# Sixteen products of zeros ahead of the third unit's scores in a fused linear-attention and gated-MLP kernel

## The chip, the cores and the metric

The program runs on one core of a Trainium2 chip. The metric is the device time of one execution in microseconds; with several runs the median is taken.

## The reference, cut to what matters

The kernel computes a linear attention with a forget gate per key channel, for 4 batches of 8 heads, 768 tokens and 48 channels, and feeds its output (4 x 768 x 384) into a gated MLP whose gate mixes tokens:

```python
f = 1.0 / (1.0 + np.exp(-f_logit))
for t in range(S):
    state = f[:, :, t, :, None] * state + np.einsum('bhd,bhe->bhde', k[:, :, t], v[:, :, t])
    y[:, :, t] = np.einsum('bhd,bhde->bhe', q[:, :, t], state)

h = np.maximum(x @ w_in, 0.0)
u, v = (h[..., :d_ff // 2], h[..., d_ff // 2:])
v_n = (v - mu) / np.sqrt(var + 1e-06)
v_s = np.einsum('ts,bsd->btd', w_spatial, v_n) + b_spatial[None, :, None]
return (u * v_s) @ w_out
```

## The kernel before, in words

The attention is cut into 24 units of 128 tokens (4 batches of 6 units), each in two chunks of 64. The order of all work is written out by hand: PLAN is a list of words such as `X:2`, and each word calls one step function with its numbers. Every engine takes its own instructions in the order in which the words stand, so a word's place sets its place in the queue of each engine that it uses.

One unit n goes through these steps. `LF`, `LK` and `LQ` load its gate logits, keys and queries, and values (lines 325 to 337, on the queue of SP); `c` clamps the logits (line 341), `e` takes exp and log (lines 345 and 346), `z` sums them along the tokens, for the first six units as products with a triangular matrix on TensorE (line 356), later as a scan on VectorE (line 351). `h` and `g` are the exponentials of the sums (lines 362 and 367), `k` and `q` scale keys and queries on VectorE (lines 373 and 377). `X` are the scores, 32 small products (line 401); `m` masks them on VectorE (line 411), `w` copies their other half on ScalarE (line 407). `YS` and `kv` are products with the values (lines 453 and 425), `r0`, `r1` and `r2` update the state (lines 433, 439 and 444), `Yq` adds the state's part of the output (line 465), `ys` copies the output (line 468), `xt` transposes it on TensorE with three products (line 477), and `xh` and `xl` split it into two parts (lines 487 and 492). The buffers of a unit's logits, keys and queries go round in threes, so that unit 6 may be loaded only when unit 3's scores have been read.

Beside the units the plan loads and splits the weights (`LV`, `LU`, `LW`, `ca`, `ct`, `ch`, `cl`, `wh`, `wl`), and from unit 4 on it weaves in the products of the MLP (`V`, `U`, `S`, `P`, `O`; lines 513, 619, 633, 664 and 818).

The word `D:n` issues n products of `junk` with itself on TensorE: `junk` is a tile of bf16 zeros set at the start, each product is 128 by 128 by 256, and its result goes to the bank that `W0` takes and `W1` gives back; nobody reads it. Each product comes with a load of its weights. The plan before has `D:11`, `D:29` and `D:3` (lines 49 to 51), and `W1` stands in line 52, behind the place of the change:

```python
def step_D(count):
    for _ in range(count):
        nc.tensor.matmul(mm.of("warm")[:, 0:2 * P], junk[:, 0:P], junk[:, 0:2 * P], start=True, stop=True)
```

Around the change the words that use TensorE are, in order: `Yq:1 xt:0 X:2 xt:1 z:4 YS:2 kv:2 X:3`. VectorE has `k:2 r2:1 q:2` ahead of the scores and `m:2 wl:1,1 k:3 r0:2` behind them. SP has `LQ:4 LF:6 LK:5 LU:0` behind `X:3`.

Of the kernel before, what the change touches and what calls it, by code (L numbers as in the profile page):

```python
# [10 lines left out]
F32 = mybir.dt.float32  # L11
# [7 lines left out]
B, H, S, D = 4, 8, 768, 48  # L19
# [10 lines left out]
P = 128  # L30
KX = HD // P
KS = S // P
KG = G // P
HK = KS // 2
TH = S // 2
# [7 lines left out]
HELD = FAST[:-1]  # L43
# [5 lines left out]
    constants LF:0 LF:1 units:1 W0 c:1 c:0 e:0 units:0 D:11 LF:2 c:2 e:1 z:0 LQ:1 LV:0 g:0 z:1 LK:0 h:0 k:0 q:0 LK:1 g:1  # L49
    h:1 k:1 fm:1 D:29 q:1 LQ:0 X:0 m:0 e:2 ca:V,0 LV:1 ct:V,0 LF:3 X:1 LF:4 w:0 c:3 YS:0 LK:3 kv:0 c:4 r0:0 ca:V,1 z:2  # L50
    r1:0 w:1 LK:4 Yq:0 r2:0 m:1 YS:1 e:4 e:3 LQ:2 LK:2 ys:0 ct:V,1 ch:V,0 D:3 kv:1 LQ:3 r0:1 r1:1 z:3 g:2 fm:0 h:2 k:2
    r2:1 q:2 fm:2 h:3 g:3 cl:V,0 Yq:1 LW:1,1 xt:0 LW:2,0 X:2 LF:5 c:5 ys:1 xt:1 fm:3 W1 z:4 q:3 m:2 wh:1,1 wl:1,1 LW:1,0
    YS:2 k:3 ch:V,1 w:2 kv:2 xh:0 e:5 wh:2,0 r0:2 X:3 g:4 LU:1 LW:0,1 cl:V,1 xl:0 runs m:3 LQ:4 Yq:2 r1:2 r2:2 z:5 w:3
    LF:6 c:6 wl:2,0 LK:5 h:4 LU:0 YS:3 ys:2 kv:3 k:4 fm:4 xh:1 wh:0,1 r0:3 q:4 V:0,0 r1:3 X:4 LF:7 ca:U,1 xl:1 xt:2 w:4
    ct:U,1 m:4 g:5 Yq:3 r2:3 e:6 k:5 wh:1,0 V:0,1 z:6 h:5 xh:2 LB YS:4 kv:4 ys:3 xt:3 q:5 xl:2 vr:0,1 r0:4 r1:4 ca:U,0
    vr:0,0 X:5 LQ:5 ch:U,1 Yq:4 c:7 fm:5 wl:1,0 wl:0,1 V:0,2 r2:4 w:5 m:5 YS:5 cl:U,1 ys:4 h:6 g:6 q:6 LW:2,1 LQ:6 xh:3
    vr:0,2 xt:4 k:6 xl:3 e:7 kv:5 xh:4 nm:0,0 X:6 r0:5 LF:9 Yq:5 z:7 vc:0,2 vc:0,1 xl:4 LF:8 LQ:7 V:0,3 r1:5 ys:5 xt:5
    m:6 V:0,4 sq:0,2 c:9 ct:U,0 sq:0,1 c:8 vc:0,0 xh:5 xl:5 sq:0,0 LW:0,0 h:7 YS:6 fm:7 na:0,0 nb:0,0 ch:U,0 V:0,5 q:7
    nc:0,0 g:7 w:6 k:7 kv:6 X:7 cl:U,0 vh:0,2 r0:6 Yq:6 vh:0,0 vl:0,0 U:0,0,3 vl:0,2 m:7 e:8 z:8 r1:6 vh:0,1 vl:0,1
    vr:0,4 bs:0,4 vr:0,3 U:0,1,3 w:7 ur:0,1,3 r2:6 YS:7 fm:6 vr:0,5 bs:0,3 bs:0,5 ys:6 na:0,1 h:8 q:8 kv:7 e:9 U:0,0,2  # L60
    r0:7 LF:10 nb:0,1 nc:0,1 ur:0,0,3 vn:0,5 xt:6 g:8 k:8 r1:7 wh:2,1 U:0,0,0 vn:0,3 LQ:8 wh:0,0 U:0,0,1 vn:0,4 c:10 X:8
    fm:8 xh:6 xl:6 vh:0,3 wl:0,0 vl:0,3 vh:0,4 Yq:7 V:1,0 ys:7 w:8 vh:0,5 m:8 vl:0,4 YS:8 vl:0,5 kv:8 ur:0,0,2 vr:1,0
    r2:7 z:9 xt:7 LF:11 LQ:9 xh:7 xl:7 h:9 r0:8 g:9 wl:2,1 e:10 r1:8 S:0,0,2 moe sg:0,0,2 LO:1 r2:8 k:9 q:9 S:0,0,1
    ur:0,0,1 Yq:8 bs:1,0 vs:1,0 ys:8 fm:9 z:10 h:10 sg:0,0,1 X:9 g:10 xt:8 sm:0,0,1 V:1,1 m:9 k:10 YS:9 w:9 q:10
    sh:0,0,1 kv:9 r0:9 X:10 ca:O,1 Yq:9 S:0,0,3 ys:9 LF:13 c:11 e:11 xh:8 r1:9 xl:8 V:1,2 r2:9 vr:1,1 LF:12 S:0,1,3
    ct:O,1 ch:O,1 sl:0,0,1 z:11 sm:0,0,2 ur:0,0,0 sg:0,0,3 m:10 fm:10 sm:0,0,3 LQ:11 xt:9 LQ:10 h:11 g:11 k:11 S:0,0,0
    vr:1,2 sg:0,1,3 q:11 bs:1,2 c:12 w:10 YS:10 kv:10 X:11 r0:10 Yq:10 cl:O,1 LO:0 m:11 sh:0,0,2 e:12 w:11 S:0,1,0 r1:10
# [87 lines left out]
def tile_kernel(ctx, tc, fkq, fn, vv, w_cv, w_spT, b_sp, out):  # L155
    nc = tc.nc
# [6 lines left out]
    pairs = pair_pool.enter_context(tc.tile_pool(name="pairs", bufs=1, space=PSUM, reuse_waits="tile"))  # L163
    dram = ctx.enter_context(tc.tile_pool(name="dram", bufs=1, space=bass.MemoryType.DRAM))
    held_v = {(b, u): dram.tile([P, G], F32, name=f"held_v{b}{u}") for b in HELD for u in range(NU)}
    held_u = {(b, th, c): dram.tile([P, TH], F32, name=f"held_u{b}{th}{c}") for b in HELD for th in range(2) for c in range(KG)}

    def tiles(pool, name, count, shape, dtype=F32):
        return [pool.tile(shape, dtype, name=f"{name}{i}") for i in range(count)]
# [17 lines left out]
    runs = attn.tile([DP, J * T], F32, name="runs")  # L187
# [735 lines left out]
    with tc.If(n_bad > 0, preferred_fallthrough_block=True, label="again"):  # L923
        xd = dram.tile([B, HD, S], F32, name="xd")
        with tc.tile_pool(name="steps", bufs=2) as sp:
# [5 lines left out]
            with tc.For_i(0, B) as b:  # L931
                for j, e in ((j, e) for j in range(J) for e in range(2)):
                    f, k, q = (sp.tile([D, NU, T], F32, tag="in", name="in", bufs=3) for _ in range(3))
# [7 lines left out]
                    f, k, q = (t.rearrange("d u t -> d (u t)") for t in (f, k, q))  # L941
# [10 lines left out]
                    for d in range(D):  # L952
                        kv = sp.tile([D, S], F32, name="kv")
# [96 lines left out]
```

## Time and profile before

| | us |
|---|---|
| median of 3 runs | 345.08 (344.42 to 346.0) |
| profiled execution, its own time | 346.77 |
| its span, first to last instruction | 345.3 |
| TensorE busy with products in the span | 330.2 (96%) |
| VectorE busy | 248.9 (72%) |
| ScalarE busy | 186.5 (54%) |
| GpSimd busy | 130.7 (38%) |

Times in the trace are counted from the first instruction. PE is TensorE, DVE VectorE, ACT ScalarE, POOL GpSimd and SP the queue that issues the transfers. The granted clock of TensorE is given as a share of full speed; it has two levels, 1.2 and 2.4 GHz, so 0.50 is the low one and a value between them is a stretch with both. The record of the clock holds its changes, and shows 1.00 ahead of the first one.

### The profile page before, as it was taken

What the parts mean: (1) busy time and instruction counts of PE and PEld (TensorE: products, weight loads), DVE (VectorE), ACT (ScalarE), POOL (GpSimd) and SP (SyncE); (2) the same over time, 40 slices, a digit from 0 to 9 for tenths busy, and PEclk for the clock granted to TensorE, in tenths of its full rate; (3) what the DMA queues carried; (4) which work ended last, traced back from release to release, by engine and by line L of the source; (5) the groups of instructions that cost most, each with busy time, mean ns of one, the idle gap of its engine ahead of it and who ended that gap; (6) DMA issues with size and microseconds to landing.
All of it is one profiled execution on the core that took longest, in us unless ns stands there. A gap on an engine that the chain in (4) does not pass through costs nothing.

```text
span 345.3 us, 10672 instructions
## 1 busy us (share of the span) xinstructions
PE 330.2 (96%) x4535; PEld 303.5 (88%) x4535; DVE 248.9 (72%) x474; ACT 186.5 (54%) x391; POOL 130.7 (38%) x128
## 2 busy tenths in 40 slices
PE   6859999999999999999999999899999999999995
PEld 5647777988999889899888999799999999999995
DVE  2677999998667876768859798977859595773420
ACT  7566799885455476558678464422344144341242
POOL 3113344313055243824235073148341466930500
PEclk9996999999999999999999999999999999999999
DMA  6978937334621839455674384451111022100022
GB/s 222 311 261 245 344 113 252 116 118 123 235 88 30 285 121 332 168 201 163 248 245 146 119 294 150 138 169 46 48 68 47 25 91 91 48 1 25 23 91 76
DMA packets 23573, 51.07 MB, mean 148 GB/s; under 512 B 2400, under 2 KB 14944, under 8 KB 23520
## 3 DMA queue, kind: packets, MB, share of 16 engines
q1 hardware_dynamic: 23520, 50.34, 43.4%
q8 instruction: 36, 0.59, 0.7%
q14 instruction: 17, 0.14, 0.1%
HBM read 39.32 MB, written 11.01 MB: 146 GB/s over the span
## 4 chain that ended last, share of the span: by engine, by line
PE 81%; DVE 7%; DMA 6%; ACT 2%; issue 1%; SPq 1%; POOL 1%; DVEq 0%; ACTq 0%; POOLq 0%
PE mm L619 11%; PE mm L513 10%; PE bank L818 10%; PE mm L664 8%; PE mm L818 7%; PE mm L633 6%; PE bank L664 6%; PE bp L401 6%; DMA fkq<-fkq 4%; PE bp L453 4%; PE bank L619 3%; PE bp L465 3%; PE mm L477 3%; PE bp L425 2%; PE bank L513 2%; DMA val<-vv 1%
## 5 line engine op out<-in xcount | busy, mean ns | idle before, releaser
L649 POOL TENSOR_TENSOR uT<-gt,uT 128x384 f32<-128x384 f32 x21 | 24.9, 1188 | 42.1 <-DVE gt L830 22.4
L341 POOL TENSOR_SCALAR fkq<-fkq 112x512 f32<-112x512 f32 (+1 forms) x15 | 24.6, 1640 | 42.8 <-DMA fkq<-fkq 24.1
L373 DVE SCALAR_TENSOR_TENSOR fkq<-fkq 112x512 f32<-112x512 f32 x24 | 19.1, 796 | 11.7 <-DMA fkq<-fkq 7.1
L401 PE MATMUL bp<-q,fkq 48*64 48x112 f32 x768 | 24.4, 266 | 2.7 <-DVE q L377 2.3
L657 DVE TENSOR_TENSOR gl<-uT,gh 128x384 fp32r<-128x384 f32 x27 | 15.9, 603 | 12.4 <-ACT gh L653 12.3
L401 PEld LDWEIGHTS bp<-q,fkq 48*64 48x64 f32 x768 | 19.7, 137 | 5.2 <-DVE q L377 3.0
L351 DVE TENSOR_TENSOR_SCAN fkq<-runs,fkq 112x512 f32<-112x512 f32 x18 | 22.1, 1230 | 2.1 <-ACT fkq L346 2.0
L444 POOL TENSOR_TENSOR sA<-sA,F 112x192 f32<-112x192 f32 x11 | 8.8, 804 | 37.9 <-DVE sA L439 25.8
L453 PEld LDWEIGHTS bp<-val,sc 64*64 64x64 f32 x768 | 14.0, 137 | 8.0 <-issue 4.4
L572 POOL TENSOR_SCALAR vr_fast<-vr_fast,mv,rs 128x512 f32<-128x512 f32 x7 | 17.7, 2529 | 8.8 <-DVE rs L567 5.4
L411 DVE TENSOR_TENSOR sc<-bp,mask 128x512 f32<-128x512 f32 x24 | 16.4, 684 | 4.7 <-PE bp L401 2.9
L653 ACT CAST gh<-uT 128x384 fp32r<-128x384 f32 x27 | 13.4, 512 | 11.7 <-POOL uT L649 8.0
L407 ACT COPY W<-bp 128x384 f32<-128x384 f32 x24 | 11.4, 474 | 14.2 <-DVE sc L411 13.3
L619 PE MATMUL mm<-xTh,w_inh 128*128 128x384 f32 x75 | 18.9, 360 | 0.0
L513 PE MATMUL mm<-w_inh,xTh 128*128 128x512 f32 x60 | 18.3, 413 | 0.0
L345 ACT ACTIVATE fkq<-fkq 112x512 f32<-112x512 f32 (+1 forms) x24 | 14.5, 606 | 6.8 <-POOL fkq L341 4.1
L453 PE MATMUL bp<-val,sc 64*64 64x48 f32 x768 | 17.0, 226 | 1.3 <-ACT W L407 0.7
L362 ACT ACTIVATE F<-fkq 112x512 f32<-112x512 f32 x18 | 11.4, 634 | 11.4 <-DVE fkq L351 6.5
L468 ACT COPY ysb<-bp 128x384 f32<-128x384 f32 x24 | 11.5, 477 | 11.0 <-PE bp L465 7.5
L619 PE MATMUL mm<-xTh,w_inl 128*128 128x384 f32 x75 | 17.1, 336 | 0.0
L619 PE MATMUL mm<-xTl,w_inh 128*128 128x384 f32 x75 | 17.1, 336 | 0.0
L513 PE MATMUL mm<-w_inh,xTl 128*128 128x512 f32 x60 | 17.0, 392 | 0.0
(245 smaller groups left out, 985.1 us busy)
## 6 DMA issues: line engine op xcount, KB each, us to landing
fkq<-fkq SPq DMA_DIRECT2D x18, 768.0 KB, 5.1
val<-vv SPq DMA_DIRECT2D x24, 192.0 KB, 5.0
out<-osb SPq DMA_DIRECT2D x24, 192.0 KB, 2.0
words<-w_cv SPq DMA_DIRECT2D x4, 768.0 KB, 8.2
fkq<-fkq SPq DMA_DIRECT2D x6, 512.0 KB, 7.1
held_u<-uT SPq DMA_DIRECT2D x15, 192.0 KB, 4.2
uT<-held_u SPq DMA_DIRECT2D x12, 192.0 KB, 2.5
held_v<-vr SPq DMA_DIRECT2D x7, 256.0 KB, 5.4
```

The lines of the kernel that those rows point to most:

```text
L341: other("c", n, nc.vector).tensor_scalar(f, f, -LOGIT_MOST, None, op0=ALU.max)
L351: return nc.vector.tensor_tensor_scan(f[0:DP], runs, f[0:DP], 0.0, op0=ALU.mult, op1=ALU.add)
L373: other("k", n, nc.vector).scalar_tensor_tensor(k, f, 1.0 / F_LEAST, k, op0=ALU.min, op1=ALU.mult)
L401: nc.tensor.matmul(sc[to, e, cs], k[dr, at:at + C], qs[n % 2][dr, j, chunk], start=True, stop=True)
L453: nc.tensor.matmul(y[to, e, cs], s[rows, keys[e]], v[rows, hd], start=j == 0, stop=False, skip_group_check=True)
L513: nc.tensor.matmul(acc, xs[:, c, ut * P:(ut + 1) * P], ws[:, c, G:FF], start=i == 0, stop=i == 3 * KX - 1)
L572: other("vn", (b, u), nc.vector).tensor_scalar(vr, vr, mean(b, th)[:, ut, 0:1], scale(b, th)[:, ut:ut + 1], op0=ALU.subtract, op1=ALU.mult)
L619: nc.tensor.matmul(acc[:, 0:TH], ws[:, kx, cs], xs[:, kx, :], start=i == 0, stop=i == 3 * KX - 1)
L633: nc.tensor.matmul(acc[:, 0:TH], vns.of((b, ks))[va][:, cs], w_sp_s[wb][:, ks, th * TH:(th + 1) * TH], start=i == 0, stop=i == 3 * KS - 1,)
L649: nc.gpsimd.tensor_tensor(uT, gts.of((b, th, c)), uT, op=ALU.mult)
L664: nc.tensor.matmul(acc[:, 0:DM], gs.of((b, th, c))[ga][:, ts], w_out_s[wb][:, c, :], start=c == cs[0] != LAST_C and ga == wb == 0, stop=c ...
L818: nc.tensor.matmul(acc, vns.of(user(i))[va][:, cs], w(i)[wb], start=n == 0 and k in (1, 2, 7), stop=n == 3 * HK - 1, skip_group_check=True)
```

## The change

`D:16` is put into the plan between `LW:2,0` and `X:2`, so on TensorE behind `xt:0` and ahead of the scores of unit 2, the third unit. The diff also makes the dictionary of DRAM buffers `held_u` for one batch more; those tiles are never written or read. Everything else of the diff is the same words in lines broken anew.

```diff
-    r2:1 q:2 fm:2 h:3 g:3 cl:V,0 Yq:1 LW:1,1 xt:0 LW:2,0 X:2 LF:5 c:5 ys:1 xt:1 fm:3 W1 z:4 q:3 m:2 wh:1,1 wl:1,1 LW:1,0
+    r2:1 q:2 fm:2 h:3 g:3 cl:V,0 Yq:1 LW:1,1 xt:0 LW:2,0 D:16 X:2 LF:5 c:5 ys:1 xt:1 fm:3 W1 z:4 q:3 m:2 wh:1,1 wl:1,1
...
-    held_u = {(b, th, c): dram.tile([P, TH], F32, name=f"held_u{b}{th}{c}") for b in HELD for th in range(2) for c in range(KG)}
+    held_u = {(b, th, c): dram.tile([P, TH], F32, name=f"held_u{b}{th}{c}") for b in range(B - 1) for th in range(2) for c in range(KG)}
```

## Rows read from the trace of the kernel before

**Rows 1.** The page: busy time by engine, and the granted clock in 40 slices.

```profile
PE 330.2 (96%) x4535; PEld 303.5 (88%) x4535; DVE 248.9 (72%) x474; ACT 186.5 (54%) x391; POOL 130.7 (38%) x128
...
PEclk9996999999999999999999999999999999999999
```

**Rows 2.** Waits of PE, whole span: total us, times, longest us.

```profile
PE mm L818 <- DVE t3l L740: 1.1, 1, 1.1
...
PE mm L477 <- ACT ysb L468: 0.5, 1, 0.5
...
PE bp L425 <- issue: 0.3, 1, 0.3
```

**Rows 3.** Chain that ended last: start us, us, what.

```profile
32.33 6.15 DMA fkq<-fkq
...
50.15 1.00 PE bp L401 x32
```

**Rows 4.** Stretches: us, busy PE PEld DVE ACT POOL, PEclk, DMA share, GB/s.

```profile
24.40:24.60 0.20, 0.00 (x0) 0.00 (x0) 0.20 (x2) 0.00 (x0) 0.00 (x0) 0.69 0.52 184
...
25.40:31.20 5.80, 5.80 (x111) 4.86 (x115) 3.81 (x5) 4.53 (x9) 2.44 (x4) 0.50 0.86 256
31.20:31.40 0.20, 0.20 (x20) 0.20 (x16) 0.00 (x0) 0.20 (x1) 0.00 (x0) 0.74 0.97 369
```

**Rows 5.** Timeline of PE, 23 to 32 us: start, us, line, tiles, count [idle before].

```profile
23.91 0.38 PE L477 MATMUL mm<-ident,ysb 128*128 128x128 f32 x2 [1.12 <-issue]
25.34 1.77 PE L401 MATMUL bp<-q,fkq 48*64 48x112 f32 x32 [1.05 <-DVE q L377]
27.04 0.90 PE L477 MATMUL mm<-ident,ysb 128*128 128x128 f32 x3
27.87 1.97 PE L356 MATMUL mm<-tri,fkq 128*64 128x128 f32 x16
29.77 1.11 PE L453 MATMUL bp<-val,sc 64*64 64x48 f32 x32
30.66 0.82 PE L425 MATMUL bp<-val,W 64*48 64x48 f32 x32
31.30 0.96 PE L401 MATMUL bp<-q,fkq 48*64 48x112 f32 x32
```

**Rows 6.** Timeline of PE, the same steps of later units at the full clock.

```profile
32.64 1.09 PE L356 MATMUL mm<-tri,fkq 128*64 128x128 f32 x16
34.40 0.68 PE L453 MATMUL bp<-val,sc 64*64 64x48 f32 x32 [0.68 <-ACT W L407]
34.91 0.54 PE L425 MATMUL bp<-val,W 64*48 64x48 f32 x32
...
37.65 1.00 PE L401 MATMUL bp<-q,fkq 48*64 48x112 f32 x32
38.58 0.55 PE L477 MATMUL mm<-ident,ysb 128*128 128x128 f32 x3
```

**Rows 7.** Timeline of PE, the first 12 us.

```profile
2.34 2.53 PE L892 MATMUL mm<-junk 128*128 128x256 bf16 x11 [2.34 <-DVE rescale L231]
5.13 3.17 PE L356 MATMUL mm<-tri,fkq 128*64 128x128 f32 x32 [0.26 <-ACT fkq L346]
8.23 3.34 PE L892 MATMUL mm<-junk 128*128 128x256 bf16 x29
```

**Rows 8.** Timeline of DVE, 27 to 32 us.

```profile
27.18 0.69 DVE L411 TENSOR_TENSOR sc<-bp,mask 128x512 f32<-128x512 f32 x1 [0.42 <-PE bp L401]
...
28.65 0.99 DVE L373 SCALAR_TENSOR_TENSOR fkq<-fkq 112x512 f32<-112x512 f32 x1
31.55 0.36 DVE L433 TENSOR_TENSOR sB<-bp,sA 112x192 f32<-112x192 f32 x1 [1.91 <-PE bp L425]
```

**Rows 9.** The stretch behind unit 3's scores, columns as in rows 4.

```profile
32.00:32.60 0.60, 0.60 (x44) 0.58 (x36) 0.60 (x1) 0.08 (x1) 0.00 (x0) 1.00 0.40 86
```

**Rows 10.** The page: queues, packets, MB, share of 16 engines.

```profile
q8 instruction: 36, 0.59, 0.7%
```

More of the change, by code (lines that the diff above doesn't have):

```diff
@@ L51 @@
     r1:0 w:1 LK:4 Yq:0 r2:0 m:1 YS:1 e:4 e:3 LQ:2 LK:2 ys:0 ct:V,1 ch:V,0 D:3 kv:1 LQ:3 r0:1 r1:1 z:3 g:2 fm:0 h:2 k:2
-    r2:1 q:2 fm:2 h:3 g:3 cl:V,0 Yq:1 LW:1,1 xt:0 LW:2,0 X:2 LF:5 c:5 ys:1 xt:1 fm:3 W1 z:4 q:3 m:2 wh:1,1 wl:1,1 LW:1,0
-    YS:2 k:3 ch:V,1 w:2 kv:2 xh:0 e:5 wh:2,0 r0:2 X:3 g:4 LU:1 LW:0,1 cl:V,1 xl:0 runs m:3 LQ:4 Yq:2 r1:2 r2:2 z:5 w:3
-    LF:6 c:6 wl:2,0 LK:5 h:4 LU:0 YS:3 ys:2 kv:3 k:4 fm:4 xh:1 wh:0,1 r0:3 q:4 V:0,0 r1:3 X:4 LF:7 ca:U,1 xl:1 xt:2 w:4
-    ct:U,1 m:4 g:5 Yq:3 r2:3 e:6 k:5 wh:1,0 V:0,1 z:6 h:5 xh:2 LB YS:4 kv:4 ys:3 xt:3 q:5 xl:2 vr:0,1 r0:4 r1:4 ca:U,0
@@ L56 @@
[L56 to L64, printed above, removed]
+    r2:1 q:2 fm:2 h:3 g:3 cl:V,0 Yq:1 LW:1,1 xt:0 LW:2,0 D:16 X:2 LF:5 c:5 ys:1 xt:1 fm:3 W1 z:4 q:3 m:2 wh:1,1 wl:1,1
@@ new lines @@
+    LW:1,0 YS:2 k:3 ch:V,1 w:2 kv:2 xh:0 e:5 wh:2,0 r0:2 X:3 g:4 LU:1 LW:0,1 cl:V,1 xl:0 runs m:3 LQ:4 Yq:2 r1:2 r2:2
+    z:5 w:3 LF:6 c:6 wl:2,0 LK:5 h:4 LU:0 YS:3 ys:2 kv:3 k:4 fm:4 xh:1 wh:0,1 r0:3 q:4 V:0,0 r1:3 X:4 LF:7 ca:U,1 xl:1
+    xt:2 w:4 ct:U,1 m:4 g:5 Yq:3 r2:3 e:6 k:5 wh:1,0 V:0,1 z:6 h:5 xh:2 LB YS:4 kv:4 ys:3 xt:3 q:5 xl:2 vr:0,1 r0:4 r1:4
+    ca:U,0 vr:0,0 X:5 LQ:5 ch:U,1 Yq:4 c:7 fm:5 wl:1,0 wl:0,1 V:0,2 r2:4 w:5 m:5 YS:5 cl:U,1 ys:4 h:6 g:6 q:6 LW:2,1
+    LQ:6 xh:3 vr:0,2 xt:4 k:6 xl:3 e:7 kv:5 xh:4 nm:0,0 X:6 r0:5 LF:9 Yq:5 z:7 vc:0,2 vc:0,1 xl:4 LF:8 LQ:7 V:0,3 r1:5
@@ new lines @@
+    ys:5 xt:5 m:6 V:0,4 sq:0,2 c:9 ct:U,0 sq:0,1 c:8 vc:0,0 xh:5 xl:5 sq:0,0 LW:0,0 h:7 YS:6 fm:7 na:0,0 nb:0,0 ch:U,0
+    V:0,5 q:7 nc:0,0 g:7 w:6 k:7 kv:6 X:7 cl:U,0 vh:0,2 r0:6 Yq:6 vh:0,0 vl:0,0 U:0,0,3 vl:0,2 m:7 e:8 z:8 r1:6 vh:0,1
+    vl:0,1 vr:0,4 bs:0,4 vr:0,3 U:0,1,3 w:7 ur:0,1,3 r2:6 YS:7 fm:6 vr:0,5 bs:0,3 bs:0,5 ys:6 na:0,1 h:8 q:8 kv:7 e:9
+    U:0,0,2 r0:7 LF:10 nb:0,1 nc:0,1 ur:0,0,3 vn:0,5 xt:6 g:8 k:8 r1:7 wh:2,1 U:0,0,0 vn:0,3 LQ:8 wh:0,0 U:0,0,1 vn:0,4
+    c:10 X:8 fm:8 xh:6 xl:6 vh:0,3 wl:0,0 vl:0,3 vh:0,4 Yq:7 V:1,0 ys:7 w:8 vh:0,5 m:8 vl:0,4 YS:8 vl:0,5 kv:8 ur:0,0,2
@@ L65 @@
+    vr:1,0 r2:7 z:9 xt:7 LF:11 LQ:9 xh:7 xl:7 h:9 r0:8 g:9 wl:2,1 e:10 r1:8 S:0,0,2 moe sg:0,0,2 LO:1 r2:8 k:9 q:9
+    S:0,0,1 ur:0,0,1 Yq:8 bs:1,0 vs:1,0 ys:8 fm:9 z:10 h:10 sg:0,0,1 X:9 g:10 xt:8 sm:0,0,1 V:1,1 m:9 k:10 YS:9 w:9 q:10
     sh:0,0,1 kv:9 r0:9 X:10 ca:O,1 Yq:9 S:0,0,3 ys:9 LF:13 c:11 e:11 xh:8 r1:9 xl:8 V:1,2 r2:9 vr:1,1 LF:12 S:0,1,3
```

## The prediction, made before the changed kernel was run

> **What bounds the kernel now.** I read the page first. TensorE is busy 330.2 us of the span of 345.3, and the granted clock is full but for one slice of the 40, the fourth [rows 1]. The list of TensorE's waits comes next: it stands still some 10 us in all, nearly all of it ahead of 50 us; behind 50 us the largest wait is 1.1 us at line 818 [rows 2]. So from 50 us on TensorE is the bound, and what an early edit is worth is what it moves of the start of unit 6's scores, at 50.15 us in the chain of waits [rows 3]. Ahead of that the chain goes through a transfer of 6.15 us from 32.33 us on, unit 6's logits, keys and queries, which is issued when unit 3's scores have been read [rows 3]. The change acts in front of that: the point to watch is the start of unit 3's scores, at 31.30 us [rows 5].
>
> The stretch around the change shows two things. TensorE ends the transposes of unit 0 at 23.91 + 0.38 = 24.29 us and waits 1.05 us for the scaled queries, until 25.34 [rows 5]. And the clock falls in this pause: the slice from 24.40 to 24.60 has a mean of 0.69, which of the two levels 1.00 and 0.50 makes a fall at 24.48 us; it is back in the slice that has 0.74, at 31.30 us, after TensorE has worked without a gap since 25.34 [rows 4, 5]. In these 6 us five steps run at the low level: scores of unit 2, transposes, sums, and the two sets of products with the values. They take 1.77 + 0.90 + 1.97 + 1.11 + 0.82 = 6.57 us [rows 5]; the same steps of later units take 1.00 + 0.55 + 1.09 + 0.68 + 0.54 = 3.86 us at the full level [rows 6], a ratio of 1.70. From the first one's start to the start of unit 3's scores they need 31.30 - 25.34 = 5.96 us, since each begins while the one before it drains; at the full level that is 5.96 / 1.70 = 3.5 us. So the low clock costs 2.5 us there, and the change can win no more than a part of it.
>
> **The change part by part.** Nothing is removed and nothing is moved on any queue but TensorE's; the extra DRAM tiles issue nothing. The added products wait for nothing: the zeros were set at the start, the bank is held already, and TensorE itself was its last writer. They do add a delay for what stands behind them on TensorE.
>
> The price of one: 29 took 3.34 us, so 0.115, and 11 at the start took 2.53 us, 0.23 each, which by the factor of two is the low level (the record of the clock shows nothing ahead of its first change) [rows 7]. A row includes the way of its last product through the array, so I take 0.11 and 0.22 us. They can start at 24.29, right behind the transposes. At the full clock sixteen take 16 x 0.11 = 1.76 us and end at 26.05, 0.7 us behind the present start of the scores; at the low one the end is later.
>
> Whether the clock still falls is the first open cost. It falls 0.19 us after the added products would begin, and TensorE had stood still for 1.12 us just ahead of the transposes [rows 4, 5]. I take it that the fall follows from what lies ahead of 24.29 and still comes at 24.48. Then 0.19 us of them run at the full level (1.7 products), and the other 14.3 take 14.3 x 0.22 = 3.15 us, to 27.63 us, if the clock doesn't rise under them. That is 2.3 us later than the scores start now.
>
> When the clock rises is the second open cost. Two rises can be read. In the stretch here it came 5.96 us after the work became gapless. At the start, 32 products of sums took 3.17 us [rows 7]; at the low level 16 of them take 1.97, 0.123 each [rows 5], at the full one 1.09, 0.068 each [rows 6]; (3.17 - 32 x 0.068) / 0.055 = 18 were slow, so the rise came at 5.13 + 18 x 0.123 = 7.35 us: 2.2 us after the pause of 0.26 us, and 5.0 after the first product of zeros [rows 7]. With the added products the gapless work begins at 24.29, so the rise would come between 24.29 + 2.2 = 26.5 and 24.29 + 6.0 = 30.25 us. The start is the nearer row, since there too zeros come first and other work follows; the mean of its two readings, 3.6 us, gives 27.9.
>
> The sum, as the start of unit 3's scores against 31.30 now:
> - rise at 27.9 (taken): the zeros end at 27.63, 0.27 us at the low level do 0.16 of the 3.5 us, and 27.9 + 3.34 = 31.24. That is 0.06 us earlier: the second half of the slow stretch is won back, and the zeros have eaten it.
> - rise at 26.5: 10.8 zeros are done by then, the rest take 0.57 us, to 27.07, and 27.07 + 3.5 = 30.57, 0.73 us earlier.
> - rise at 30.25: 2.62 us at the low level do 1.54, and 30.25 + 1.96 = 32.21, 0.91 us later.
>
> VectorE doesn't undo the taken case: unit 2's mask starts now at 27.18 and unit 3's keys end at 28.65 + 0.99 = 29.64, 2.46 us later [rows 8]. With scores that end near 28.75 the mask starts there and the keys are ready at 31.2, just when TensorE wants them. The cover is VectorE's pause of 1.91 us ahead of the state's update at 31.55 [rows 8]; gone, it would cost its excess one for one. ScalarE's copies behind the mask move by the same 1.5 us, and the products with the values wait for them only from about 30.2 us on, when the sums have ended.
>
> Behind unit 3's scores all goes on as now, so the profiled execution of 346.77 us (1.47 us more than its span) becomes 346.7. The median of the runs, 345.08, is 1.7 us below that execution; I put the difference to the median: 345.08 - 0.06 = 345.0 us.
>
> One cost lies in code. The core fetched instructions 36 times, 0.59 MB [rows 10], 16 KB each, and TensorE stood still 1.12 us in the middle of unit 0's transposes and 0.3 us at line 425 for no reason but issue [rows 2, 5]. The change adds 16 products and 16 weight loads, so a wait of that kind behind it meets the stream 32 instructions earlier, about one half of a step of 64, 0.3 to 0.5 us. Bounds are 0 and 0.3 + 0.5 = 0.8 us; the wait of 0.5 us for ScalarE at line 477 [rows 2] covers most of it, and I take 0. The Trainium skill (Runtime: NRT & Kernel Launch, Instruction fetch mechanics) says that a fetch of the next block is mostly hidden; by that the term is 0. The row of 1.12 us speaks against it, in this stretch at least.
>
> **The rivals.** First, the clock doesn't fall, since the pause is filled, or falls at another place in most executions: nothing in one trace fixes the instant, and the runs spread over 1.6 us. The zeros end at 26.05, unit 3's scores start at 29.55, 1.75 us earlier. For it: the pause of 1.05 us is gone. Against it: the 0.19 us. Not all would arrive at 50 us: the transfers ahead of unit 6's load are just ending when it is issued, since the queue's share is 0.40 from 32.00 to 32.60 [rows 9] against 0.86 before that [rows 4], so an earlier issue shares the queue with them. What surely arrives is the idle share there, some 0.4 us; at most it is 1.75. I take 0.9: 344.2 us; the end is 343.3.
>
> Second, on the other side: the clock rises no sooner than now, at 31.30, because the zeros do for it what the gapless scores did not. Then they only delay: from 27.63 to 31.30 the low level does 3.67 / 1.70 = 2.16 us of the work, and 31.30 + 1.34 = 32.64, 1.34 us later. Unit 6's load goes out so much later into an idle queue [rows 9], so all of it arrives: 346.4 us. It decides from a rise behind 28.1 us on, where the sum changes sign. With the wait for code on top it is 347.2.
>
> Third, the change does nothing that the clock or the end sees, as its delay of 0.7 us at the full clock is taken up by later pauses: 345.1.
>
> The Trainium skill (TensorE: Matmul & The Clock Gate, What's actually happening) has activity release a throttled clock. By that an earlier rise is likely, so it bears on the choice between forecast and second rival; the trace agrees in that both rises came under gapless work [rows 4, 7].
>
> **How the numbers follow.** Forecast (fall stays, earlier rise, even): 0.50. No fall: 0.25. Rise not sooner: 0.15. Nothing seen: 0.10. A difference under 0.5% (1.7 us) is about what a measurement of this kernel can't tell from none. Only the end of the first rival (343.3) is over it on the fast side, I give it 0.12 with what I overlook; on the slow side only the second rival with the wait for code, 0.08. Within lies 0.80. The range reaches from 343.6, most of the first rival, to 346.4, the second one.
>
> **What would show it.** In the profile after: the zeros start near 24.3 and end at 27.6 at 0.22 us each; the granted clock still falls near 24.5 and is back near 27.9 instead of 31.3; unit 2's scores start at 27.6, take about 1.0 us, and unit 3's start near 31.2; unit 6's load is issued near 32.3 and its scores start near 50.1. A clock that stays full through 24 to 32 us proves the first rival, one that stays low to 31 the second. The prediction is wrong if unit 6's scores move by over 1 us.

## The result: 348.08 us, and the profile after

| | before | after |
|---|---|---|
| median of 22 runs each, side by side, us | 346.0 (343.32 to 347.83) | 348.08 (345.56 to 353.38) |
| ratio of after to before | | 1.0055, 95% interval 1.003 to 1.0081 |
| profiled execution, its own time, us | 346.77 | 349.18 |
| its span, us | 345.3 | 347.7 |

The changed kernel is slower by 0.55%, 1.9 us. Executions over 1.5% above the fastest of their kernel count in the medians and not in the ratios, and the profile of one run below, `e4_late`, fell on such an execution and is not read. The forecast was no change (345.0 us, range 343.6 to 346.4).

The page of the profile after: span, busy time by engine, granted clock in 40 slices, and the queue that fetches TensorE's code.

```profile
span 347.7 us, 10704 instructions
...
PE 331.2 (95%) x4551; PEld 304.7 (88%) x4551; DVE 248.8 (72%) x474; ACT 186.6 (54%) x391; POOL 127.8 (37%) x128
...
PEclk9999999999999999999999989999999999999999
...
q8 instruction: 37, 0.61, 0.7%
```

Against [rows 1, 10]: 16 products and 16 weight loads more, a clock that no longer shows its dip in the fourth slice but a smaller one in the 24th, and one code fetch more, 37 for 36.

TensorE's timeline after, at the start (start us, us, line, tiles, count, idle before and its releaser):

```profile
21.96 0.55 PE L477 MATMUL mm<-ident,ysb 128*128 128x128 f32 x3
22.35 1.91 PE L892 MATMUL mm<-junk 128*128 128x256 bf16 x16
24.19 1.00 PE L401 MATMUL bp<-q,fkq 48*64 48x112 f32 x32
...
27.71 1.00 PE L401 MATMUL bp<-q,fkq 48*64 48x112 f32 x32
...
33.44 0.48 PE L425 MATMUL bp<-val,W 64*48 64x48 f32 x23 [1.21 <-issue]
...
47.87 1.00 PE L401 MATMUL bp<-q,fkq 48*64 48x112 f32 x32
```

The zeros take 1.91 us in all and start 0.11 us apart, and the steps behind them run at the full level: unit 2's scores take 1.00 us where they took 1.77 [rows 5]. Unit 3's scores start at 27.71 instead of 31.30, and unit 6's at 47.87 instead of 50.15. At that point the change has *won* 2.28 us in this execution. The two stretches of the clock and busy time agree (columns as in [rows 4]; the second one is the dip behind 200 us):

```profile
22.40:31.40 9.00, 7.79 (x213) 6.44 (x210) 8.50 (x14) 6.34 (x13) 3.10 (x5) 1.00 0.87 261
...
202.80:206.20 3.40, 3.40 (x14) 3.21 (x13) 1.82 (x4) 1.67 (x5) 2.80 (x2) 0.50 0.63 177
```

All of that and 2.4 us more are lost later. TensorE's waits of the whole span after, in the columns of [rows 2]:

```profile
PE mm L619 <- ACT t3h L737: 1.9, 1, 1.9
PE bp L453 <- DMA val<-vv: 1.7, 2, 1.0
PE bp L425 <- issue: 1.2, 1, 1.2
```

The first of them is new. Its place, in TensorE's timeline after:

```profile
200.07 0.55 PE L477 MATMUL mm<-ident,ysb 128*128 128x128 f32 x3
202.51 0.89 PE L619 MATMUL mm<-xTh,w_inh 128*128 128x384 f32 x3 [1.89 <-ACT t3h L737]
203.19 1.16 PE L619 MATMUL mm<-xTl,w_inh 128*128 128x384 f32 x3
```

and the same words in before, where nothing is waited for:

```profile
200.55 0.55 PE L477 MATMUL mm<-ident,ysb 128*128 128x128 f32 x3
200.85 0.78 PE L619 MATMUL mm<-xTh,w_inh 128*128 128x384 f32 x3
```

The releaser named is ScalarE's `t3h`, but the product reads `xTh` and `w_inh`, the copy ends at 202.27 us, 0.24 ahead of the restart, and the same step in before waited for no such thing. What does fit is the code queue, in the stretch from 200.0 to 200.3 us:

```profile
q8 instruction: 1, 0.02, 20.3%
```

This one packet of 16 KB begins at 200.13 us and takes 0.97; TensorE restarts 2.38 us after its begin. The waits that the profile does put down to issue have the same shape: a fetch begins at 31.15 and TensorE restarts at 33.44 (2.29), and in before one begins at 21.47, with the restart at 23.91 (2.44, [rows 5]). So I read the new wait as a wait for code.

A count bears this out. Number all of TensorE's instructions in a trace in the order of their start (products, weight loads, semaphore and control instructions; 9143 in before, 9175 in after) from 0 on, and call the numbers records. In before the two waits put down to issue end at records 705 and 1474, in after at 1217 and 1986, and the new one at 7617: each is 705 plus a multiple of 256, within one. So these are the places where one block of 256 instructions ends and the next begins, the block edges. The edge at 7617 stands in before as well, but there it falls on a later step, a weight load of line 513, which starts with this row:

```profile
203.56 0.85 PE L513 MATMUL bank<-w_inl,xTh 128*128 128x512 f32 x3
```

That is 3.33 us after the begin of the fetch at 200.23 us, and nothing waits. With 32 records more, the edge falls on the product of line 619 that in before is due at 200.85 us, too soon after the same fetch.

Behind the wait the clock falls for 3.41 us, from 202.83 to 206.24.

The account of the profiled executions, by the starts of three steps that both have (all on TensorE; `t3h` is the product of line 818 at 216.9 us in before), the last copy of the output on ScalarE, and the end:

| stretch, us | before | after | after less before |
|---|---|---|---|
| to unit 6's scores | 50.15 | 47.87 | -2.28 |
| unit 6's to unit 18's scores | 109.26 | 110.94 | +1.68 |
| unit 18's scores to `t3h` | 57.53 | 61.26 | +3.73 |
| `t3h` to the end of the last copy | 125.21 | 123.38 | -1.83 |
| last copy to the end of the span | 3.12 | 4.25 | +1.13 |
| span | 345.27 | 347.68 | +2.41 |

Line 2 is mostly the waits for values (1.7 us in two against 0.5 in one). They aren't shown to come from the change: `e6_ahead`, `e10_at161` and `e11_late_again` below have the instructions of before up to the first of them and wait 1.04, 1.93 and 0.65 us there. Line 3 is the wait of 1.89 us and the slow clock behind it. Line 4 gives back, 1.1 us of it because the wait for VectorE's `t3l` [rows 2] is gone: TensorE, being late, no longer outruns VectorE there. Line 5 is the end of the program. The last copies, in the chains of after and of before:

```profile
342.95 0.48 ACT osb L681
```

```profile
341.67 0.48 ACT osb L681
```

In before the last fetch of TensorE's code begins at 339.4 us, while its products still run. After has one at 340.6 and one more, at 344.0, when its last product has been over for 1.2 us. The count agrees: the last block edge is at record 9153 (705 + 33 x 256), and TensorE's records end 10 ahead of it in before and 22 behind it in after.

### The profile page after: what moved, and what is told of

Read it like the earlier page. It is cut to its first block, busy times and chain, and to the rows that moved or that the text cites. A ratio compares the mean times of both kernels' runs of the same rounds, so it can differ in the third digit from the quotient of the medians.

```text
span 347.7 us, 10704 instructions
## 1 busy us (share of the span) xinstructions
PE 331.2 (95%) x4551; PEld 304.7 (88%) x4551; DVE 248.8 (72%) x474; ACT 186.6 (54%) x391; POOL 127.8 (37%) x128
## 4 chain that ended last, share of the span: by engine, by line
PE 79%; DMA 9%; DVE 6%; ACT 2%; issue 2%; SPq 1%; POOL 0%; DVEq 0%; ACTq 0%; POOLq 0%
PE mm L619 11%; PE bank L818 10%; PE mm L513 10%; PE mm L664 7%; PE mm L818 7%; PE bank L664 7%; PE mm L633 6%; PE bp L401 4%; DMA fkq<-fkq 4%; PE bp L453 3%; DMA val<-vv 3%; PE bank L619 3%; PE bank L513 2%; PE bp L465 2%; PE bp L425 2%; PE mm L477 2%
## 5 line engine op out<-in xcount | busy, mean ns | idle before, releaser
L401 PE MATMUL bp<-q,fkq 48*64 48x112 f32 x768 | 23.7, 261 | 0.5 <-DVE q L377 0.3
L401 PEld LDWEIGHTS bp<-q,fkq 48*64 48x64 f32 x768 | 19.0, 133 | 3.2 <-DVE q L377 1.1
L572 POOL TENSOR_SCALAR vr_fast<-vr_fast,mv,rs 128x512 f32<-128x512 f32 x7 | 16.8, 2405 | 9.4 <-DVE rs L567 5.4
L624 ACT ACTIVATE uT<-mm 128x384 f32<-128x384 f32 x23 | 11.2, 489 | 12.7 <-PE mm L619 6.1
```

The source lines that it names most:

```text
L401: nc.tensor.matmul(sc[to, e, cs], k[dr, at:at + C], qs[n % 2][dr, j, chunk], start=True, stop=True)
L572: other("vn", (b, u), nc.vector).tensor_scalar(vr, vr, mean(b, th)[:, ut, 0:1], scale(b, th)[:, ut:ut + 1], op0=ALU.subtract, op1=ALU.mult)
```

## The experiments

In each run 9 to 12 executions of the kernel stand against 29 to 35 of the kernel before on the same chip. Three theories were tried; the expectations speak of the work, of the code or its edges, and of the count. By the first, the zeros' time and the clock in the array make the difference. By the second, 32 more instructions on TensorE move the block edges of its code, and edges come to two sensitive places (about 200 us, and the end). By the third, each added instruction costs by itself.

### Work or code

`e1_small` keeps the 32 instructions and takes the array time away, `e2_wide` has the same zeros in half as many instructions, `e3_same_code` has the full zeros at the place and saves 32 instructions at the start, `e5_less_code` makes that saving without the change.

```diff
 # e1_small: in the plan T:16 in place of D:16
+    def step_T(count):
+        for _ in range(count):
+            nc.tensor.matmul(mm.of("warm")[0:16, 0:16], junk[:, 0:16], junk[:, 0:16], start=True, stop=True)
 # the others: a second number gives products of 512 columns
+        for _ in range(wide):
+            nc.tensor.matmul(mm.of("warm"), junk[:, 0:P], junk, start=True, stop=True)
 # e2_wide:             D:16 -> D:0,8
 # e3_same_code:        D:11 -> D:5,3   D:29 -> D:3,13   (D:16 stays)
 # e5_less_code:        D:11 -> D:5,3   D:29 -> D:3,13   (no D:16)
```

> The 16 products of 256 columns are replaced by 16 products of 16 columns at the same place: the same 32 instructions on TensorE, but some 0.5 us in place of 1.8, inside a pause of 1 us. Theory CODE (32 more instructions move the places where TensorE crosses into code that is not there yet; in the profile after this is a wait of 1.9 us at 200.6 us, a clock fall behind it worth 1.1 us, and an end that is 1.1 us longer with 37 fetches in place of 36): slower than before by 1 to 3 us; 37 fetches, the last copy of the output to the end of the span 4.2 us in place of 3.1, a wait of over 1 us near 200 us. Theory WORK (the time of the products themselves, and what their clock does, is the cost): within 0.5 us of before, 36 fetches, an end as before.

> 8 products of 512 columns in place of 16 of 256: the same time on the array, half the instructions (16 more than before). CODE: the edge that meets the wait at 200.6 us comes 16 instructions later, some 1.4 us of work, so the wait shrinks from 1.9 to about 0.5 us; the end is either that of before or that of after; in time 0 to 1 us under the changed kernel's 2.1 us loss or better. WORK: as the changed kernel, 2 us slower than before.

> The changed kernel, with the 40 earlier products of zeros of 256 columns at the start made into 24 (16 of them of 512 columns): the same time on the array there, 32 instructions fewer, so that everything behind the added products stands at the same place in the code as in the kernel before. CODE: 36 fetches, an end of 3.1 us, no wait near 200 us; what the clock gives at unit 6 (up to 2.3 us) is left in part: 0.5 to 2 us faster than before. WORK: as the changed kernel, 2 us slower than before.

> The kernel before without the change, with the same merging of the products at the start: 32 instructions fewer than before, all else the same. CODE: 36 fetches or fewer, a short end, the edges come 32 instructions later; time within 1 us of before, either way, since other places meet the waits. WORK: no difference, within 0.5 us. It is the control for the merging in the kernel with the same code.

| | instructions against before | median, us (before 345.81) | ratio, 95% interval |
|---|---|---|---|
| e1_small | +32 | 347.65 | 1.0059 (1.0025 to 1.0093) |
| e2_wide | +16 | 346.64 | 1.0002 (0.9973 to 1.003) |
| e3_same_code | 0 | 345.99 | 1.0004 (0.9975 to 1.0032) |
| e5_less_code | -32 | 344.62 | 0.9952 (0.9921 to 0.9983) |

The theory of the work falls twice, within intervals of some 0.3%. With next to no array time the kernel is as slow as the changed one, and with the full zeros but the old number of instructions it is as fast as before. The profile of `e1_small`: the page's span, the tiny products at the place, the restart after a fetch that begins at 202.59 us, and the last copy, from which the end is 4.08 us away.

```profile
span 348.6 us, 10704 instructions
...
22.79 0.55 PE L896 MATMUL mm<-junk 128*16 128x16 bf16 x16
...
204.80 0.68 PE L619 MATMUL mm<-xTh,w_inh 128*128 128x384 f32 x3 [1.58 <-issue]
...
344.08 0.48 ACT osb L681
```

Here the profile itself names issue at the place where it named `t3h` in after. `e2_wide`, with 16 instructions more, lies between, as expected: its records end at 9159, behind the last edge, with 37 fetches and 3.74 us from the last copy to the end, and record 7617 falls on a later group of the same products, where it waits 0.27 us:

```profile
202.07 0.34 PE L619 MATMUL mm<-xTh,w_inl 128*128 128x384 f32 x1 [0.27 <-issue]
```

Its time doesn't show these costs (1.0002, with an interval of 0.3% either way). And `e3_same_code`: no wait at that place, 36 fetches again, and 3.20 us from the last copy to the end.

```profile
span 346.7 us, 10672 instructions
...
343.02 0.48 ACT osb L681
```

It isn't 0.5 to 2 us faster than before, though, as I had expected. In its profile TensorE waits 2.12 us for code until 35.15 us, at record 1217, the clock is low for 6.83 us from 34.51 us on, and unit 6's scores start at 51.54 us.

### The same 32 instructions elsewhere

Sixteen tiny products go into the kernel before at four places: `e9_at118` ahead of a product of line 619 at 108 us (118 in its label and expectation is wrong; the values awaited near 158 us still come behind it), `e10_at161` at 162 us, `e6_ahead` at 197 us (all ahead of the place at 200), `e4_late` and its repetition `e11_late_again` ahead of a product of line 818 at 217 us of before (behind it).

```diff
 # in step_U, (b, th, c) == (1, 0, 3) for e9_at118, (2, 0, 0) for e10_at161, (2, 1, 1) for e6_ahead
 # in step_P, (b, k, m) == (1, 7, 1) for e4_late and e11_late_again
+            for _ in range(16):
+                nc.tensor.matmul(acc[0:16, 0:16], junk[:, 0:16], junk[:, 0:16], start=True, stop=True)
```

> The kernel before with 16 products of zeros of 16 columns (32 instructions, 0.55 us) ahead of the seventh products of batch 1, at 216.9 us, just in front of a wait of 1.1 us for VectorE that covers them. CODE: nothing ahead of it moves, no wait at 200 us; one fetch more (37), the stretch from the last output copy to the end 0.5 to 1.1 us longer than the 3.1 of before; so 0.5 to 1.1 us slower. If the end is not a matter of code: within 0.4 us of before, end of 3.1 us.

> The kernel before with the same 16 small products ahead of the products of line 619 that begin at 198.2 us, so just ahead of the place of the wait at 200.6 us. Their own time is 0.55 us, uncovered. CODE: the edge comes 32 instructions earlier against the same fetch that starts at 200.2 us, so a wait of 0.7 to 1.9 us ahead of the products of line 619 at 200.9 us, ending 2.2 to 2.4 us after the fetch begins, with a fall of the clock behind it in some executions (1.1 us), and the longer end (0.5 to 1.1 us): 1.8 to 4 us slower than before. If what stands between 24 and 198 us is the cause: only their own time, 0.3 to 0.6 us slower.

> The kernel before with the 16 small products (32 instructions, 0.55 us, uncovered) ahead of the products of line 619 near 118 us: behind the first 50 us and ahead of the load at 158 us. CODE, all of it behind 118 us (a load of values that lands 1 us late behind a code fetch at 158 us, the wait at 200 us, the longer end of some 1 us): 1.5 to 2.5 us slower, as the changed kernel; a wait of 0.9 us or more ahead of line 453 near 158 us. If the first 50 us carry the changed kernel's loss: 0.5 to 1.5 us slower (own time and the end).

> The same 16 small products ahead of the products of line 619 near 161 us, so behind the load at 158 us and ahead of the place at 200 us. CODE: no added wait near 158 us, a wait of 0.3 to 1.9 us near 200 us that the wait for VectorE at 218 us takes up, the longer end of 1 us: 0.7 to 1.5 us slower, as with the small products at 198 us (0.75 us). If the wait at 158 us is not one of code: as with the products at 118 us.

> The small products at 217 us once more, for a narrower interval (it gave 1.0046 with 1.0006 to 1.0086). CODE: the longer end alone, 0.7 to 1.2 us slower, 37 fetches. If the end is covered by something: within 0.4 us of before.

| | place, us of its profile | median, us | of before | ratio, 95% interval | wait about 200 us | last copy to end |
|---|---|---|---|---|---|---|
| e9_at118 | 108 | 346.74 | 345.97 | 1.0027 (0.9995 to 1.006) | 1.91 | 4.54 |
| e10_at161 | 162 | 348.2 | 345.97 | 1.0069 (1.003 to 1.0108) | 1.61 | 3.98 |
| e6_ahead | 197 | 346.63 | 346.52 | 1.0022 (0.9982 to 1.0062) | 0.94 | 4.50 |
| e4_late | not read | 347.9 | 346.52 | 1.0046 (1.0006 to 1.0086) | not read | not read |
| e11_late_again | 214 | 346.61 | 345.97 | 1.0038 (1.0004 to 1.0071) | none | 3.87 |

The restarts of `e9_at118`, `e10_at161` and `e6_ahead` (three kernels, each its own line of TensorE's timeline):

```profile
200.86 0.68 PE L622 MATMUL mm<-xTh,w_inh 128*128 128x384 f32 x3 [1.91 <-ACT t3h L740]
```

```profile
204.47 1.12 PE L622 MATMUL mm<-xTh,w_inh 128*128 128x384 f32 x3 [1.61 <-issue]
```

```profile
201.80 0.69 PE L622 MATMUL mm<-xTh,w_inh 128*128 128x384 f32 x3 [0.94 <-ACT ysb L468]
```

The releasers are three different ones; the fetches are alike: they begin at 198.42, 202.12 and 199.44 us, and TensorE restarts 2.44, 2.35 and 2.36 us later. All three restart at record 7617, as after, `e1_small` and `e15_changed_again` do. Put ahead of the place, the instructions bring the wait there from wherever they stand; put behind it, they don't: in `e11_late_again` record 7617 starts 3.06 us after the fetch's begin, without a wait. There the longer end is left: the page has 37 fetches, and the last copy starts at

```profile
340.64 0.48 ACT osb L681
```

in a span of 345.0 us, 3.87 us to the end against 3.12. It isn't the only difference: the profile also has a wait of 0.86 us at 297 us for ScalarE's `uT_fast`, as `e9_at118` has and before and after have not, and its cause is open. The ratio of 1.0038 is 1.3 us, with an interval from 0.1 to 2.5, so it fits the longer end and can't size it.

My sizes for `e6_ahead` (1.8 to 4 us) and `e9_at118` were too large, and that for `e10_at161` (0.7 to 1.5 us, measured 2.4) too small. The wait about 200 us isn't lost as a whole: a late TensorE then doesn't wait for `t3l`, which is worth up to 1.1 us and some tenths. By estimate 0.5 us or so remains, and 1.4 us more where the clock falls behind the wait (3.41 us at the low level do the work of 2.0 at the ratio of 1.70), as it does in after and `e15_changed_again` (202.8), `e9_at118` (202.2) and `e10_at161` (204.4 us) and doesn't in `e1_small` and `e6_ahead`. I also expected no wait at 158 us in `e10_at161`, and there is one of 1.61 us, for values, though it has the instructions of before up to there.

### Zeros without more code, again

`e7_refill` is `e3_same_code` with the tiny products at the place, so neither zeros there nor more code; `e8_wide_all` makes all zeros wide; `e12_less_again` repeats `e5_less_code`.

```diff
 # e7_refill:     D:11 -> D:5,3   D:29 -> D:3,13   T:16 at the place of D:16
 # e8_wide_all:   D:11 -> D:1,5   D:29 -> D:1,14   D:3 -> D:1,1   D:16 -> D:0,8
```

> The merged products at the start (32 instructions fewer), and 16 small products in place of the 16 added ones (32 instructions more): code behind that place as before, none of the added array time. CODE: as the kernel before and as the kernel with the same code and the full products, within 0.5 us of both; 36 fetches, no wait at 200 us. If the merging itself makes the gain of the kernel with less code (345.81 to 344.62): 1.2 us faster than before. If the added products of 256 columns are worth something by their clock: slower than the kernel with the same code (345.99).

> The added zeros as 8 products of 512 columns, and all 43 earlier products of 256 columns made into 23 (20 of 512): the same array time as the changed kernel, 24 instructions fewer than the kernel before behind the added place. CODE: 36 fetches, no wait at 200 us, a short end; between the kernel with less code (344.62) and before (345.81). WORK (array time and the clock): as the kernel with the same code, no gain over before.

> The kernel with 32 instructions fewer once more, against these runs of before (it gave 0.9952 with 0.9921 to 0.9983). CODE: 0.5 to 1.7 us faster, 36 fetches, no wait of TensorE at 158 or 200 us. If the first result was chance: within 0.4 us of before.

| | instructions against before | median, us | of before | ratio, 95% interval | last copy to end |
|---|---|---|---|---|---|
| e7_refill | 0 | 345.98 | 346.52 | 1.0008 (0.9972 to 1.0044) | 3.26 |
| e8_wide_all | -24 | 345.37 | 346.52 | 0.9983 (0.995 to 1.0016) | 3.47 |
| e12_less_again | -32 | 345.02 | 345.97 | 0.9973 (0.9937 to 1.001) | 3.36 |

`e3_same_code` and `e7_refill` have the same code positions, one with real zeros at the place and one with next to none, and they can't be told apart, within intervals of 0.3 to 0.4%. So what the zeros do to the clock at 24 us is worth nothing that can be measured at the end. None of the three has the wait about 200 us, all have 36 fetches. The kernels with fewer instructions come out lowest, `e5_less_code` and its repetition `e12_less_again` at 0.9952 and 0.9973. It is the best version here and beats the changed kernel; against before the first run is clear of noise, and the second's interval just includes no difference. Where the gain of 0.9 to 1.7 us comes from isn't settled; their ends (3.35 and 3.36 us) are like that of before, and no stretch of their profiles is shorter by so much in both.

### A whole block more

If edges decide, 256 instructions more ahead of unit 2's scores should put all edges behind it back, with one fetch more. `e13_block` does so with the kernel before, `e14_changed_block` with the changed one; `e15_changed_again` runs the changed kernel beside them.

```diff
 # e13_block:          D:11 -> D:0,4 T:20   D:29 -> D:0,10 T:60   T:28 ahead of Yq:0   T:16 ahead of Yq:1   T:30 ahead of X:2
 # e14_changed_block:  the same without T:30, with D:16 and T:74 in place of T:60
```

> The kernel before with 128 products of zeros more in all (256 instructions, one whole block of code), small ones of 16 columns put into the pauses of the first 25 us and in place of some of the zeros there. EDGE (the place of the edges counts): behind 25 us the edges stand as in the kernel before, so an end of 3.1 to 3.5 us though there are 37 fetches, no wait of code at 200 us; within 1 us of before, either way, by what the first 25 us do. COUNT (each added instruction or fetch counts): 256 instructions cost eight times what 32 do, over 5 us slower, and a long end.

> The changed kernel, with its 16 added products of 256 columns, filled up in the same manner to 256 instructions over before. EDGE: as the kernel before and as the one with the same code, within 1 us of before, an end of 3.1 to 3.5 us with 37 fetches, so 1 to 2 us faster than the changed kernel. COUNT: slower than the changed kernel by 5 us or more.

> The changed kernel itself, beside the two above. Both theories: 1.0055 of before within its interval (1.003 to 1.008), 37 fetches, an end of 3.7 to 4.6 us.

| | instructions against before | median, us (before 345.81) | ratio, 95% interval | wait about 200 us | last copy to end |
|---|---|---|---|---|---|
| e13_block | +256 | 347.54 | 1.0056 (1.0024 to 1.0088) | none | 3.12 |
| e14_changed_block | +256 | 348.43 | 1.006 (1.0025 to 1.0096) | none | 3.13 |
| e15_changed_again | +32 | 348.16 | 1.0067 (1.0034 to 1.0099) | 1.99 | 3.62 |

The places came out as the theory of the edges has it. In `e14_changed_block` and `e13_block` the stretch from unit 18's scores to the end takes 186.5 and 186.2 us, as in before (185.86); in after and `e15_changed_again` it takes 188.88 and 188.24. There are 37 fetches, as in after, but the last one begins at 340.6 us in `e13_block`, ahead of the last copy (342.86) as in before, and the records (9399) end again 10 ahead of an edge. So it isn't one fetch more that lengthens the end, but where the last one falls. TensorE's timeline of `e13_block`, where after has its wait of 1.89 us:

```profile
201.53 0.55 PE L477 MATMUL mm<-ident,ysb 128*128 128x128 f32 x3
201.83 0.78 PE L619 MATMUL mm<-xTh,w_inh 128*128 128x384 f32 x3
```

and of `e15_changed_again`, with a fetch that begins at 199.64 us:

```profile
202.06 0.69 PE L619 MATMUL mm<-xTh,w_inh 128*128 128x384 f32 x3 [1.99 <-ACT t3h L737]
```

The times didn't: I expected both within 1 us of before, and they are 1.9 and 2.1 us behind it. In their profiles the loss lies ahead of unit 18's scores, which start at 160.3 and 160.5 us, against 158.4 in `e15_changed_again` and 159.4 in before. By unit 6's scores `e14_changed_block` is 3.3 us behind `e15_changed_again` (49.83 against 46.57), which is no more than the spread of kernels with the same instructions up to there (below), and a wait of 1.05 us follows at 62.4 us, put down to ScalarE's `vr`. `e13_block` waits 0.89 us at the same product and `e15_changed_again` 0.37; in the block kernels it is record 2510, 13 behind an edge, so the count doesn't make it a wait for code. That the filling itself is in the way ahead of unit 18, which also puts fewer columns of zeros at the start than before has, is argued, not shown. The count falls as a theory in its simple form: by it, 256 instructions would cost eight times 1.9 us. That any larger change of the instructions costs some 2 us is not excluded by the times of these two runs, only made unlikely by where their profiles lose it and by `e3_same_code` and `e7_refill`.

## Why the prediction was wrong

**The step that failed is the code term.** The prediction priced the 32 instructions at 0, with 0.8 us as the upper bound, from the row of 1.12 us and that of 0.3 [rows 2, 5], and looked only at the stretch next to the change. The 32 instructions shift every block edge of the 300 us behind them. Two of those edges came to bad places, neither near the change: record 7617, with the wait of 1.89 us about 200 us, and record 9153, with the fetch behind the last product. The trace of before could have told the first one: its two waits for code give the edges, the fetch begins at 200.23 us, a restart comes some 2.4 us after a begin, and the product on which the edge then falls is due at 200.85, so a wait of some 1.8 us. The runs size the two so. The end: 3.62 to 4.54 us from the last copy in the seven profiles read of kernels with 32 instructions more (mean 4.12), against 3.12 to 3.47 in the six with none more or fewer (mean 3.29), so 0.8 us. The wait about 200 us, by the estimate above: 0.5 us behind `t3l`, and 1.4 us more when the clock falls. Together that is 1.3 to 2.7 us; measured are 1.9 us for the change and 2.3 for its repetition, and 0.8 to 2.4 us for the five kernels in which the same number of instructions stands elsewhere. The Trainium skill (Runtime: NRT & Kernel Launch, Instruction fetch mechanics) calls the crossing of a block of 16 KiB, 256 instructions, mostly hidden. The size of the blocks agrees with the page's row (0.61 MB in 37 packets); "mostly hidden" holds for most of the 37 (in after TensorE stands still for three, 1.21, 0.26 and 1.89 us), and not for the two that decide here.

**That the fall at 24.48 us still comes was wrong too.** The clock stayed full from 22.4 to 31.4 us, which is the first rival. The code ahead of the zeros is the same, but the fetch that split unit 0's transposes began at 21.47 us in before and at 19.29 in after; the transposes start at 21.96 in one piece, and there is no pause of 1.12 us for a fall to follow. That this is why the clock stayed isn't shown. Unit 3's scores were 3.59 us earlier where that rival gave 1.75: 2.44 from the clock, and 1.15 because unit 2's scores start at 24.19 and not at 25.34.

**That what is won at unit 6's scores arrives at the end was wrong,** and it was the frame of the whole sum. After starts them 2.28 us earlier and ends 2.41 us later; at unit 18's scores 0.6 us of the lead was left, since TensorE had waited for values in between. And the start itself is no figure of the code: before, `e6_ahead`, `e9_at118`, `e10_at161` and `e11_late_again` have the same instructions up to there, and unit 6's scores start at 50.15, 48.13, 47.13, 48.04 and 46.09 us. My row of 50.15 was the latest of five. The fall of the clock that I costed, 6.83 us from 24.48 us on, came at 23.54 us in `e10_at161`; in `e6_ahead` and `e9_at118` 3.41 us from 26.27 and 31.55 us on stand in its place, and in `e11_late_again` no fall came. So the lead of 2.28 us may be in part or in whole the luck of two executions. A sum to a hundredth of a microsecond on one such execution had no ground.

**What held.** The products' price (0.11 us each at the full level), the bank and the queues that nothing else waits for, and the price of the early clock, 2.5 us: from unit 2's to unit 3's scores after takes 3.52 us, where I gave 3.5, against 5.96. The second rival, the one on the slow side, was named for the wrong reason: a clock that rises late. Its addition "with the wait for code" (347.2 us) was the nearest in kind, with the wait put at the wrong place.

**What stays open.** Why the kernel with 32 instructions fewer gains 0.3 to 0.5%; how much of the loss of `e13_block` and `e14_changed_block` is their filling; and why the loads of values issued near 155 us land later in some kernels (4.7 to 4.9 us after their issue in after, `e1_small` and `e2_wide`, 3.3 to 4.0 in before and `e5_less_code`). The code packet seems to hold them back: in after, `e1_small`, `e2_wide`, `e9_at118`, `e10_at161` and `e15_changed_again` the wait for values near 158 us ends 1.94 to 1.95 us after the end of a code packet, whether that took 0.96 or 2.10 us. No run was made for it.

## What to carry to other kernels

In a long unrolled program an added instruction has a second price, at every place behind it where the engine can't stand a late block of code: number the engine's instructions in the trace of before, find the edges from its waits for code, and ask which of them would move into a tight stretch or past the last product. A filler should be few wide instructions, not many narrow ones, and its effect should be tested against the same number of instructions with no work in them. Take the start of an early step from several executions before costing an edit at its distance to it.

## What the runs showed of the hardware that I had not expected

- A fetch of TensorE's code is one packet of 16 KB that takes 0.88 to 2.10 us in the profiles read. From 20 us on the 16 profiles read have 25 waits of 0.26 to 2.12 us, in 14 of them, that are put down to issue or end at record 7617. After every one TensorE restarts 1.2 to 1.5 us behind the end of such a packet, 2.2 to 2.8 behind its begin, and within one record of 705 plus a multiple of 256 (in `e7_refill` and `e8_wide_all`, whose traces lack one and three records, when these are added).
- The profile may put such a wait down to another engine (`t3h` in after, `e9_at118` and `e15_changed_again`, `ysb` in `e6_ahead`, issue in `e1_small` and `e10_at161`) though it is at one place with one cause; the code queue's packet tells it.
- A fetch that falls behind the last product goes with an end of the program that is 0.5 to 1.4 us longer than the 3.12 us of before.
- A pause of 1.6 to 2.0 us in the middle of the program can be followed by 3.41 us at the low level, 1.2 GHz, or by none (`e1_small` kept 1.00 behind 1.58 us, `e10_at161` behind 1.93 us near 116 us).
